# A set-attention and mixture-of-experts kernel: a listed order, output weights in the x buffers, later outputs of two batches, small steps on ScalarE or GpSimd

## The chip, the cores and the metric

The kernel runs on one core of one Trainium2 chip. The metric is device microseconds (us) of one execution, the median of several. Engines are called by the names of the profile: PE (TensorE), DVE (VectorE), ACT (ScalarE), POOL (GpSimd) and SP (SyncE, whose queue issues the transfers).

## The reference

`x` is 4 batches of 11456 tokens with 128 channels in float32, `inducing` is 32 rows of 128 channels. What is computed, cut to what matters:

```
def mab(q, kv):
    s = scale * (q @ kv.transpose(0, 2, 1))
    s = s - s.max(-1, keepdims=True)
    a = np.exp(s)
    a /= a.sum(-1, keepdims=True) + 1e-09
    return a @ kv
h = mab(I, x)             # 32 inducing rows attend over all tokens of a batch
out = mab(x, h)           # every token attends over the 32 rows h
# then, with x = out as 45824 rows:
do_compute = x @ w_skip > 0
e_idx = argmax(x @ w_gate); gate_w = softmax(x @ w_gate)[e_idx]
out[do_compute] = x + gate_w * (relu(x @ w1[e_idx]) @ w2[e_idx])
```

## The kernel before, in words

Tokens lie along the free dimension, channels on the 128 partitions. A batch is cut into six groups g0 to g5 of 2048 tokens (the short one has 1216; it comes first in batch 0 and last in the others), and a group into four quarters (`Q`), so that a tile of 128 partitions holds four quarters of 32 inducing rows. For each batch b there are these steps:

- **load** (L372): SP issues two transfers of 512 KB for each group of x.
- **first pass**, for each pair of groups: scores (L403, PE), their maximum (L407, DVE), exponentials (L413, ACT), transposes of these weights (L422, PE) and a copy out of PSUM; transposes of x (L438, PE, 8 at a time) and a copy (`xt`, on ACT at L354 or on DVE at L356); the weighted sum of x (L452, PE), added up on DVE (L461).
- **middle**, once in a batch, a chain of small steps: L504 to L534 make the normalised `hr` (L527 is its matmul, L532 the reciprocal before it), L537 transposes it, L543 copies it as `hc`; from `hc` come the logits of the 32 rows (L553, L554), the batch's expert (`choose`, L563 to L568), `lrq` (`seven`, L599 to L605), and through the expert's weights (`w1s`, `w2s`, loaded by SP after it has read the expert's number) `g` (L613, L620), signs (L635 to L639) and `yr` (L657 to L672).
- **second pass**, for each pair of groups, here called a unit: scores with `hc` (L754, PE), 32x32 block transposes into `e` (L758, DVE), softmax (L762 and L777 on DVE, L773 on ACT; `less` L770 and `norm` L783 as two halves on DVE or POOL), a transpose back into `u1` (L789); the expert's logits (L797, PE; `lt`, L806 and L807, DVE), `qexp` (L812, L813, ACT), `claim` (L817 to L820, POOL), the gates (L825, L826 on DVE, `pick` L829 on POOL, L834 on PE, a copy `gs` on ACT or DVE), `scale2` (L845, halves on DVE or POOL) and a second transpose back into `u2` (L789).
- **emit**, for each group: 8 matmuls with `hr` and `u1` and 8 with `yr` and `u2` (L885, PE, into two PSUM pairs), two copies `o` (ACT, or DVE), two stores (L894, SP). Below, one emit is a full one (2048 tokens) or a short one (1216).
- **marking** (L915 to L942), small, feeds a check at the end that decides whether tokens with another expert have to be added; in the profiled execution it found nothing to add.

No engine reorders its work. What stands in which order is made when the kernel is built: every step is an `Op` with a cost on each engine that may run it, buffers that it takes and frees, and a rank. `in_order` is a list scheduler: it goes through the steps by the time at which they could start, takes the lowest rank first among those within 0.1 us, picks the engine that would end first, and hands out the buffers. `best_order` starts from ranks by formula (for a group, `b * NG + g`, for its second pass `LEAD` more) and tries 4000 random changes of them, keeping what ends earlier by the planner's costs. The program is written in the order found; the waits come from the buffers. Where the planner sees PE idle for over 0.7 us, `awake` and `idle` put in transposes of the identity that nobody reads (L1124), which I call fillers.

Buffers: 11 for x (one holds a group), 3 for `u1`, 1 for `u2`, 4 for `o`, and five PSUM homes, three of which are pairs.

Of the kernel before, what the change touches and what calls it, by code (L numbers as in the profile page):

```python
# [22 lines left out]
HOMES = (2, 2, 2, 1, 1)  # L23


class Group:
# [1149 lines left out]
```

## Time and profile before

| | |
|---|---|
| median of 3 runs | 223.78 us (223.65 to 223.88) |
| the profiled execution | 222.58 us |
| its span, first to last instruction | 220.6 us |
| PE, DVE, ACT, POOL busy | 90%, 73%, 59%, 39% of the span |
| last matmul ends | 212.5 us |
| last store issued | 214.6 us |

The busy share is a mean over stages with different limits, so the stages are to be read one by one; a good cut are the four `hr` matmuls (L527), at 37.45, 74.22, 114.75 and 165.70 us of the span. PE's share counts the fillers as work.

### The profile page before, as it was taken

What the parts mean: (1) busy time and instruction counts of PE and PEld (TensorE: products, weight loads), DVE (VectorE), ACT (ScalarE), POOL (GpSimd) and SP (SyncE); (2) the same over time, 40 slices, a digit from 0 to 9 for tenths busy, and PEclk for the clock granted to TensorE, in tenths of its full rate; (3) what the DMA queues carried; (4) which work ended last, traced back from release to release, by engine and by line L of the source; (5) the groups of instructions that cost most, each with busy time, mean ns of one, the idle gap of its engine ahead of it and who ended that gap; (6) DMA issues with size and microseconds to landing.
All of it is one profiled execution on the core that took longest, in us unless ns stands there. A gap on an engine that the chain in (4) does not pass through costs nothing.

```text
span 220.6 us, 6196 instructions
## 1 busy us (share of the span) xinstructions
PE 199.2 (90%) x2535; PEld 125.6 (57%) x2536; DVE 161.1 (73%) x330; ACT 129.9 (59%) x183; POOL 86.7 (39%) x156
## 2 busy tenths in 40 slices
PE   6899999999999999999999989999988999786840
PEld 5478767764666876854657555445734236652420
DVE  0135306799999788288799998899998999999400
ACT  2365564716769855966948473566956553165650
POOL 6000000026285207333631576418672572983400
PEclk9999999999999999999999999999999999999996
DMA  6999950089920459909988937445227796008693
GB/s 161 398 416 408 408 237 0 3 278 413 408 87 3 192 132 386 360 7 361 352 297 269 357 144 243 195 189 229 83 95 288 223 390 265 0 24 360 247 348 110
DMA packets 16613, 51.63 MB, mean 234 GB/s; under 512 B 1984, under 2 KB 4928, under 8 KB 16576
## 3 DMA queue, kind: packets, MB, share of 16 engines
q1 hardware_dynamic: 16288, 51.12, 61.8%
q8 instruction: 22, 0.36, 0.7%
q14 instruction: 15, 0.12, 0.2%
q10 hardware_dynamic: 288, 0.02, 0.1%
HBM read 27.68 MB, written 23.46 MB: 232 GB/s over the span
## 4 chain that ended last, share of the span: by engine, by line
PE 42%; DVE 37%; DMA 5%; ACT 5%; issue 5%; POOL 3%; SPq 1%; ACTq 0%; DVEq 0%; POOLq 0%
PE bank L438 12%; PE bank L885 7%; DVE u L789 7%; PE bank L403 6%; PE bank L754 5%; DVE sums L777 5%; PE bank L452 4%; DVE e L758 3%; PE bank L422 3%; DMA x<-in_xT_dram 3%; DVE ts L762 3%; DMA out_dram<-o 2%; DVE mins L407 2%; DVE e L783 2%; DVE lt L806 1%
## 5 line engine op out<-in xcount | busy, mean ns | idle before, releaser
L354 ACT COPY o<-bank 128x1024 f32<-128x1024 f32 (+1 forms) x45 | 41.5, 954 | 15.9 <-PE bank L885 13.4
L438 PE MATMUL bank<-ident,x 128*128 128x128 f32 (+1 forms) x368 | 48.8, 277 | 1.0 <-DMA x<-in_xT_dram 0.5
L354 ACT COPY xt<-bank 128x1024 f32<-128x1024 f32 (+1 forms) x41 | 40.4, 996 | 15.8 <-PE bank L438 15.5
L438 PEld LDWEIGHTS bank<-ident,x 128*128 128x128 f32 (+1 forms) x368 | 40.6, 140 | 7.0 <-issue 2.4
L770 POOL TENSOR_TENSOR e<-e,ts 128x512 f32<-128x512 f32 (+1 forms) x19 | 20.6, 1093 | 58.3 <-DVE ts L762 58.3
L407 DVE TENSOR_REDUCE mins<-bank 128x1 f32<-128x1024 f32 (+3 forms) x13 | 13.7, 1056 | 23.4 <-PE bank L403 23.3
L789 DVE STREAM_TRANSPOSE u<-e 128x1024 f32<-128x1024 f32 (+1 forms) x24 | 28.3, 1186 | 2.8 <-PE bank L885 1.5
L783 POOL TENSOR_TENSOR e<-texp,ts 128x512 f32<-128x512 f32 (+1 forms) x19 | 20.2, 1073 | 23.0 <-DVE ts L779 15.0
L885 PE MATMUL bank<-u,hr 32*128 32x512 f32 (+1 forms) x192 | 26.0, 611 | 1.3 <-ACT o L354 1.1
L452 PE MATMUL bank<-xt,a1T 128*32 128x129 f32 (+1 forms) x736 | 25.3, 275 | 0.1
L452 PEld LDWEIGHTS bank<-xt,a1T 128*32 128x32 f32 (+1 forms) x736 | 19.5, 109 | 9.1 <-issue 6.3
L885 PE MATMUL bank<-u,yr 32*128 32x512 f32 (+1 forms) x192 | 23.5, 558 | 0.0
L403 PE MATMUL bank<-x,iT_sb 128*32 128x512 f32 (+1 forms) x192 | 22.8, 566 | 0.3 <-DMA x<-in_xT_dram 0.2
L754 PE MATMUL bank<-x,hc 128*32 128x512 f32 (+1 forms) x192 | 22.1, 578 | 1.0 <-DVE e L758 0.5
L413 ACT ACTIVATE a<-bank,mins 128x1024 f32<-128x1024 f32 (+3 forms) x13 | 13.0, 997 | 15.0 <-DVE mins L410 12.3
L845 POOL TENSOR_TENSOR e<-e,gs 128x512 f32<-128x512 f32 (+1 forms) x15 | 17.2, 1158 | 6.9 <-ACT gs L354 5.8
L773 ACT ACTIVATE texp<-e 128x1024 f32<-128x1024 f32 (+1 forms) x12 | 12.4, 1030 | 8.4 <-POOL e L770 8.4
L777 DVE TENSOR_REDUCE sums<-texp 128x32 f32<-128x1056 f32 (+1 forms) x12 | 14.3, 1195 | 3.6 <-ACT texp L773 3.5
L354 ACT COPY a1T<-bank 128x1024 f32<-128x1024 f32 (+4 forms) x17 | 12.1, 735 | 6.8 <-PE bank L422 6.7
L758 DVE STREAM_TRANSPOSE e<-bank 128x1024 f32<-128x1024 f32 (+1 forms) x12 | 14.3, 1190 | 1.6 <-PE bank L754 1.2
L885 PEld LDWEIGHTS bank<-u,yr 32*128 32x128 f32 x192 | 9.8, 185 | 9.4 <-issue 7.8
L817 POOL TENSOR_SCALAR posm<-lt 128x32 f32<-128x32 f32 (+1 forms) x12 | 4.2, 353 | 24.8 <-DVE lt L806 24.8
(131 smaller groups left out, 262.9 us busy)
## 6 DMA issues: line engine op xcount, KB each, us to landing
x<-in_xT_dram SPq DMA_DIRECT2D x43, 512.0 KB, 8.4
out_dram<-o SPq DMA_DIRECT2D x40, 512.0 KB, 3.4
out_dram<-o SPq DMA_DIRECT2D x8, 304.0 KB, 4.4
w1s<-in_w_dram SPq DMA_DIRECT2D x4, 512.0 KB, 3.9
w2s<-in_w_dram SPq DMA_DIRECT2D x4, 512.0 KB, 5.0
x<-in_xT_dram SPq DMA_DIRECT2D x4, 152.0 KB, 2.7
x<-in_xT_dram SPq DMA_DIRECT2D x3, 96.0 KB, 5.2
iT_sb<-in_iT_dram ACTq DMA_DIRECT2D x1, 16.0 KB, 2.2
```

The costliest lines, as they stand in the source:

```text
L354: nc.scalar.copy(out=out, in_=in_)
L403: nc.tensor.matmul(ps[q * M:(q + 1) * M, off[i]:off[i] + G.w1], lhsT=iT_sb, rhs=s.x[g][:, G.s1[q]:G.s1[q] + G.w1], start=True, stop=True)
L407: nc.vector.tensor_reduce(out=bias if one else mins[:, 0:1], in_=st["ps"][:, 0:W], axis=AX.X, op=ALU.max, negate=True)
L438: nc.tensor.transpose(out=px[0:w, (j * Q + q) * P:(j * Q + q + 1) * P], in_=s.x[gs[i]][:, o:o + w], identity=ident)
L452: nc.tensor.matmul(ph[q * M:(q + 1) * M, 0:P + 1], lhsT=st["aT"][0:w, j, q * M:(q + 1) * M], rhs=xts[bx[i].idx][0:w, k, q, :], start=(j == ...
L754: nc.tensor.matmul(ps[q * M:(q + 1) * M, off[i]:off[i] + G.w2], lhsT=s.hc[:, 0:M], rhs=s.x[g][:, G.s2[q]:G.s2[q] + G.w2], start=True, stop ...
L758: nc.vector.transpose(out=st["e"], in_=st["ps"][:, 0:W])
L770: on(o).tensor_tensor(out=v, in0=v, in1=part(st["mx"], i), op=ALU.subtract)
L777: nc.vector.tensor_reduce(out=r, in_=ev(M + 1), axis=AX.X, op=ALU.add)
L783: on(o).tensor_tensor(out=blocks(st["e"], i), in0=texps[bex.idx][:, t0:t0 + Gs[i].nb, 0:M], in1=part(st["i"], i), op=ALU.mult)
L789: nc.vector.transpose(out=st[f"u{k}"][:, 0:W], in_=st["e"])
L885: nc.tensor.matmul(at(bp[q // 2])[:, p0:p0 + G.w1], lhsT=m[r, :], rhs=st[k][r, c], start=(k == "u1"), stop=(k == "u2"))
```

## The change

- The order is no longer searched. `placed` reads a rank, and for steps with a choice of engine a bias, from a list of numbers, one for each step (`RANKS`), and runs `in_order` once. It overwrites every rank that the formulas give, those with `LEAD`, `EL` and `LATE` too, so these constants have no effect of their own.
- The four `u` buffers are gone and there are 13 x buffers. A unit takes one x buffer for its `u1` and `u2` when `u1` is written and gives it back after its last emit. The planner hands out x buffers one by one (`rooms`) rather than in turn.
- The emits of the last two batches have a rank of their own (`LE`).
- Small steps: `dw` is one ACT instruction with a negated bias from POOL (L521 on DVE goes); the scaling of `hr`, the copies `hc`, `g`, `yp`, `yr` may run on ACT; `seven` has four instructions rather than five and may run on POOL; the row sum of `hc` is a step by itself, so that the second pass doesn't wait for it; `unsure` has one instruction less; `least` is a tensor_tensor.
- The short group's quarters of 304 tokens are cut into blocks of 102, 100 and 102 rather than 128, 128 and 48, and transposed 102 at a time.
- Fillers are written right before the step that follows the gap rather than behind the step ahead of it. On PE this is the same place.

```diff
-def best_order(ops, bufs, rounds):
...
+def placed(ops, bufs):
+    table = RANKS.split()
+    assert len(table) == len(ops)
+    for o, v in zip(ops, table):
+        rank, _, spare = v.partition("/")
+        o.rank, o.spare = int(rank) / 100.0, int(spare or 0) / 10.0
+    done, end = in_order(ops, bufs)
+    assert end < math.inf
+    return done
...
+            elif b.tag == "x":
+                ends = [0.0 if v is None else v.end for v in rooms]
+                lo = min(v for v in ends if v is not None)
+                b.idx = max((v, i) for i, v in enumerate(ends) if v is not None and v <= max(t, lo))[1]
+                rooms[b.idx] = b
...
-        self.tb = [(c, min(P, self.w1 - c)) for c in range(0, self.w1, P)]
+        n = -(-self.w1 // P)
+        self.wb = -(-self.w1 // n)
+        at = [min(c, self.w1 - self.wb) for c in range(0, n * self.wb, self.wb)] + [self.w1]
+        self.tb = [(c, d - c) for c, d in zip(at, at[1:])]
...
-    XB = min(11, 2 * NG)
+    XB = min(13, 2 * NG + 2)
-    LEAD = NG + 4
+    LEAD = NG + 1
-    BUFS = {"x": XB, "a1": 2, "a1T": 1, "xt": 2, "e": 3, "u1": 3, "u2": 1, "lt": 2, "o": 4, "w": 1, "gsel": 1, "ex": 2}
+    BUFS = {"x": XB, "a1": 2, "a1T": 1, "xt": 2, "e": 3, "lt": 2, "o": 4, "w": 1, "gsel": 1, "ex": 2}
+    LATE = B - 2
+    EL = 4
...
-            nc.vector.tensor_tensor(out=d, in0=st["bb"][:, 0:1], in1=s.bias, op=ALU.subtract)
...
+            nc.scalar.activation(out=d, in_=st["bb"][:, 0:1], func=AF.Exp, bias=st["top"])
...
-            nc.vector.tensor_copy(out=s.hc[:, 0:P], in_=pt[:, 0:P])
-            nc.vector.tensor_reduce(out=s.hc[:, P:P + 1], in_=pt[:, 0:M], axis=AX.X, op=ALU.add)
-        s.o_hc = o = L.add({"DVE": 0.5}, columns, o, free=[f])
+            copy(o, s.hc[:, 0:P], pt[:, 0:P])
+        def whole(o):
+            nc.vector.tensor_reduce(out=s.hc[:, P:P + 1], in_=s.hc[:, 0:M], axis=AX.X, op=ALU.add)
+        s.o_hc = o = L.add({"DVE": 0.28, "ACT": 0.29}, columns, o, free=[f])
+        o = L.add({"DVE": 0.25}, whole, o)
...
-        s.o_lrq = L.add({"DVE": 0.89}, seven, o)
+        s.o_lrq = L.add({"DVE": 0.75, "POOL": 1.3}, seven, o)
...
-        b1, b2 = Buf("u1"), Buf("u2")
+        bu = Buf("x")
+        LE = Steps(L.rank + (EL if b >= LATE else 0))
...
+            u = st[f"u{k}"] = xs[bu.idx][:, (k - 1) * PW:k * PW]
+            nc.vector.transpose(out=u[:, 0:W], in_=st["e"])
...
-            o = emit(s, g, G, off[i], st, L, (o_1, o_2, o), [b1, b2] if i == len(gs) - 1 else [])
+            o = emit(s, g, G, off[i], st, LE, (o_1, o_2, o), [bu] if i == len(gs) - 1 else [])
...
-        done = best_order(all_steps(), BUFS, 4000)
+        done = placed(all_steps(), BUFS)
```

Where instructions now stand, at three places. In the rows, `hr_1_...` is `hr` of batch 1 and so on; in the changed kernel `u1` and `u2` are called x, since they lie in x buffers; L942 there is L885 of before, L891 is L834, L854 is L797, L1180 is L1124.

PE behind the transpose of batch 3's `hr`, up to the first scores of its second pass, before:

```order
L537 MATMUL bank3_73<-ident_80,hr_3_2270 128x128
L885 MATMUL bank2_72<-u1_2_2_1987,hr_2_1615 128x512 x2
L885 MATMUL bank0_70<-u1_2_2_1987,hr_2_1615 128x512 x2
L885 MATMUL bank2_72<-u2_2_2_2252,yr_2_1901 128x512 x2
L885 MATMUL bank0_70<-u2_2_2_2252,yr_2_1901 128x512 x2
L553 MATMUL bank4_74<-ws_sb_78,hc_3_2288 128x8
L554 MATMUL bank4_74<-ws_sb_78,hc_3_2288 128x9
L754 MATMUL bank1_71<-x_3_0_1459,hc_3_2288 32x512 x4
```

and in the changed kernel:

```order
L594 MATMUL bank4_71<-ident_77,hr_3_2138 128x128
L942 MATMUL bank2_69<-x6_154,hr_1_1031 128x304 x2
L942 MATMUL bank0_67<-x6_154,hr_1_1031 128x304 x2
L942 MATMUL bank2_69<-x6_154,yr_1_1280 128x304 x2
L942 MATMUL bank0_67<-x6_154,yr_1_1280 128x304 x2
L982 MATMUL bank3_70<-lom_2_2136,ones_82 128x1
L613 MATMUL bank4_71<-ws_sb_75,hc_3_2159 128x8
L614 MATMUL bank4_71<-ws_sb_75,hc_3_2159 128x9
L942 MATMUL bank2_69<-x9_157,hr_1_1031 128x512 x2
L942 MATMUL bank1_68<-x9_157,hr_1_1031 128x512 x2
L942 MATMUL bank2_69<-x9_157,yr_1_1280 128x512 x2
L942 MATMUL bank1_68<-x9_157,yr_1_1280 128x512 x2
```

Before, batch 2's third group is emitted here and batch 1 is long done; now a short and a full emit of batch 1 stand here. Counted to the end of the order, 10 emits stood behind this place (4 of batch 2, one of them short, and 6 of batch 3, one short), and now 15 do (3 of batch 1, one short, and 6 each of batches 2 and 3, one short each).

PE around the gates of batch 3's first unit, before:

```order
L797 MATMUL bank1_71<-u1_3_0_2306,lrq_3_163 32x128 x8
L668 MATMUL bank3_73<-yp_3_2481,rep_100 128x128
L1124 MATMUL bank2_72<-ident_80 128x128 x41
L834 MATMUL bank3_73<-lt_3_0_2472,rep_100 32x32 x4
L797 MATMUL bank3_73<-u1_3_2_2377,lrq_3_163 32x128 x8
L1124 MATMUL bank2_72<-ident_80 128x128 x15
L885 MATMUL bank0_70<-u1_3_0_2306,hr_3_2270 128x512 x2
```

and in the changed kernel:

```order
L854 MATMUL bank4_71<-x11_159,lrq_3_173 32x128 x8
L726 MATMUL bank3_70<-yp_3_2355,rep_97 128x128
L942 MATMUL bank0_67<-x1_149,hr_2_1632 128x512 x2
L942 MATMUL bank2_69<-x1_149,hr_2_1632 128x512 x2
L942 MATMUL bank0_67<-x1_149,yr_2_1880 128x512 x2
L942 MATMUL bank2_69<-x1_149,yr_2_1880 128x512 x2
L1180 MATMUL bank3_70<-ident_77 128x128 x7
L942 MATMUL bank0_67<-x1_149,hr_2_1632 128x304 x2
L942 MATMUL bank1_68<-x1_149,hr_2_1632 128x304 x2
L942 MATMUL bank0_67<-x1_149,yr_2_1880 128x304 x2
L942 MATMUL bank1_68<-x1_149,yr_2_1880 128x304 x2
L891 MATMUL bank4_71<-lt_3_0_2373,rep_97 32x32 x4
```

Where 41 fillers stood, a full and a short emit of batch 2 and 7 fillers stand now. In the whole program the fillers go from 78 to 32, not counting the 13 that both have ahead of the first transfer.

ACT in the last unit of batch 3, from `qexp` to the copy of the gates, before:

```order
L812 ACTIVATE qexp1_124<-lt_3_4_2636 128x28x7
L813 ACTIVATE qexp1_124<-qexp1_124 128x28x7
L354 COPY o_3_2_0_2674<-bank0_70 128x1024
L354 COPY gs2_1_148<-bank3_73 128x28
L354 COPY o_3_2_1_2683<-bank1_71 128x1024
```

and in the changed kernel:

```order
L869 ACTIVATE qexp1_121<-lt_3_4_2521 128x28x7
L870 ACTIVATE qexp1_121<-qexp1_121 128x28x7
L401 COPY o_3_1_0_2560<-bank0_67 128x1024
L401 COPY o_3_1_1_2566<-bank1_68 128x1024
L401 COPY o_3_2_0_2588<-bank0_67 128x1024
L401 COPY gs2_1_145<-bank4_71 128x28
```

One output copy stood ahead of the last gates, and now three do.

## Rows read from the trace of the kernel before

**Rows 1.** The page: busy time of the engines over the span, then the slices of PE, of its granted clock and of the transfers (40 slices of 5.5 us, tenths).

```profile
PE 199.2 (90%) x2535; PEld 125.6 (57%) x2536; DVE 161.1 (73%) x330; ACT 129.9 (59%) x183; POOL 86.7 (39%) x156
...
PE   6899999999999999999999989999988999786840
...
PEclk9999999999999999999999999999999999999996
DMA  6999950089920459909988937445227796008693
```

**Rows 2.** Busy time of each engine between the four `hr` matmuls, from the first matmul on x to the end; the columns are stretch, length, busy time (and instructions) of PE, its weight loads, DVE, ACT and POOL, then granted clock, share of the transfer engines, GB/s.

```profile
4.40:37.45 33.05, 32.09 (x403) 21.33 (x403) 10.61 (x19) 17.72 (x25) 0.00 (x0) 1.00 0.81 320
37.45:74.22 36.77, 36.26 (x516) 24.69 (x513) 33.50 (x70) 23.72 (x34) 15.72 (x21) 1.00 0.50 191
74.22:114.75 40.53, 39.80 (x548) 26.07 (x547) 30.39 (x67) 27.18 (x37) 15.86 (x23) 1.00 0.74 266
114.75:165.70 50.95, 48.28 (x646) 29.00 (x644) 48.24 (x94) 33.36 (x48) 26.66 (x39) 1.00 0.54 201
165.70:212.50 46.80, 39.93 (x424) 21.63 (x420) 38.35 (x82) 25.10 (x35) 24.90 (x39) 1.00 0.61 232
212.50:220.60 8.10, 0.00 (x0) 0.00 (x0) 0.00 (x0) 1.33 (x2) 0.00 (x0) 0.79 0.54 194
```

**Rows 3.** PE's timeline from batch 3's `hr` matmul to the end (start, length, then the instructions; in brackets the idle time before).

```profile
165.70 0.49 PE L527 MATMUL bank<-acc,rep 128*128 128x129 f32 x2
...
168.11 1.14 PE L885 MATMUL bank<-u,hr 32*128 32x512 f32 x8
...
170.04 0.39 PE L553 MATMUL bank<-ws_sb,hc 128*128 128x8 f32 x2
...
180.40 0.79 PE L885 MATMUL bank<-u,hr 32*128 32x304 f32 x8 [0.48 <-ACT o L354]
...
181.64 0.44 PE L626 MATMUL bank<-ident,g 128*128 128x128 f32 x2
...
185.89 4.64 PE L1124 MATMUL bank<-ident 128*128 128x128 f32 x41
191.10 0.27 PE L834 MATMUL bank<-lt,rep 128*32 128x32 f32 x8 [0.57 <-POOL lt L829]
```

**Rows 4.** Groups of instructions by line and shape over the whole span (count, busy time, mean of one in ns, then idle time before).

```profile
L354 ACT COPY o<-bank 128x1024 f32<-128x1024 f32 x37 | 36.3, 1016 | 13.5 <-PE bank L885 12.2 <-issue 1.2
...
L1124 PE MATMUL bank<-ident 128*128 128x128 f32 x78 | 9.9, 276 | 0.0
...
L845 POOL TENSOR_TENSOR e<-e,gs 128x512 f32<-128x512 f32 x12 | 14.4, 1200 | 6.2 <-ACT gs L354 5.0 <-DVE gs L356 1.1
...
L845 DVE TENSOR_TENSOR e<-e,gs 128x512 f32<-128x512 f32 x8 | 8.6, 1069 | 1.5 <-ACT gs L354 1.5
...
L356 DVE COPY xt<-bank 128x1024 f32<-128x1024 f32 x5 | 6.1, 1225 | 2.1 <-PE bank L438 2.1
...
L356 DVE COPY o<-bank 128x1024 f32<-128x1024 f32 x3 | 3.6, 1197 | 0.2 <-PE bank L885 0.2
...
L783 DVE TENSOR_TENSOR e<-texp,ts 128x512 f32<-128x512 f32 x3 | 2.9, 973 | 0.0
...
L620 DVE COPY g<-bank 128x256 f32<-128x256 f32 x4 | 1.6, 399 | 0.0
...
L605 DVE TENSOR_TENSOR lrq<-r,cmask 128x32 f32<-128x32 f32 x4 | 1.4, 338 | 0.2
...
L665 DVE COPY yp<-bank 128x128 f32<-128x128 f32 x4 | 1.1, 287 | 1.9 <-PE bank L834 1.4 <-PE bank L657 0.5
```

**Rows 5.** Busy time, columns as in the second group, in three stretches of the end: from batch 3's reciprocal (L532) to its first `e` transpose (L758), from there to the last `lt` (L806), and from there to the end of the last `u2` transpose (L789).

```profile
167.24:173.74 6.50, 5.89 (x57) 2.75 (x61) 5.43 (x27) 3.33 (x6) 3.37 (x9) 1.00 0.66 250
173.74:201.95 28.21, 23.88 (x265) 13.69 (x261) 27.30 (x42) 13.63 (x19) 17.75 (x24) 1.00 0.54 198
201.95:208.20 6.25, 4.79 (x51) 2.20 (x47) 4.05 (x13) 4.07 (x7) 3.79 (x8) 1.00 0.72 290
```

**Rows 6.** The last unit's gates, from the timeline of all engines: POOL's `pick` (L829), its matmul (L834), the copy of the gates, DVE's half of `scale2` (L845), and the two marking steps (L938, L939) that POOL runs behind the pick.

```profile
204.21 0.48 POOL L829 TENSOR_TENSOR lt<-lt,gs 128x112 f32<-128x112 f32 x1 [0.32 <-DVE gs L826]
204.66 0.46 POOL L938 TENSOR_SCALAR gxs<-gxs 128x96 f32<-128x96 f32 x1
204.75 0.16 PEld L834 LDWEIGHTS bank<-lt,rep 128*32 128x32 f32 x8 [2.11 <-POOL lt L829]
...
205.08 0.18 ACT L354 COPY gs<-bank 128x28 f32<-128x28 f32 x1 [0.57 <-PE bank L834]
...
205.19 0.39 POOL L939 TENSOR_TENSOR gxs<-gxs,posm 128x96 f32<-128x96 f32 x1
205.29 0.83 DVE L845 TENSOR_TENSOR e<-e,gs 128x512 f32<-128x512 f32 x1 [1.22 <-ACT gs L354]
```

**Rows 7.** The x loads (the line L372), time from issue to landing.

```profile
DMA to landing us min/median/max: 2.3/8.0/11.3
```

**Rows 8.** The granted clock of PE around the end of its work, columns as in the second group.

```profile
214.00:216.00 2.00, 0.00 (x0) 0.00 (x0) 0.00 (x0) 0.59 (x1) 0.00 (x0) 1.00 0.78 280
216.00:218.00 2.00, 0.00 (x0) 0.00 (x0) 0.00 (x0) 0.00 (x0) 0.00 (x0) 0.80 0.57 197
218.00:220.60 2.60, 0.00 (x0) 0.00 (x0) 0.00 (x0) 0.00 (x0) 0.00 (x0) 0.50 0.03 9
```

More of the change, by code (lines that the diff above doesn't have):

```diff
@@ L298 @@
     xts = [const.tile([P, GC // Q // P, Q, P + 1], F32, name=f"xt{i}") for i in range(BUFS["xt"])]
+    xs = [const.tile([P, GC], F32, name=f"x{i}") for i in range(XB)]
     for t in xts:
@@ L389, in first @@
         tb = [(i, k, c, w) for i, G in enumerate(Gs) for k, (c, w) in enumerate(G.tb)]
-        nt, full = len(tb), sum(w == P for *_, w in tb)
+        nt = len(tb)
+        runs = [(sum(len(H.tb) for H in Gs[:i]), len(G.tb), G.wb) for i, G in enumerate(Gs)]
+        if n == 2 and Gs[0].wb == Gs[1].wb:
+            runs = [(0, nt, Gs[0].wb)]
         mins = None if one else s.mins
@@ L409, in least @@
         def least(o):
[L410 removed]
+            nc.vector.tensor_tensor(out=bias, in0=mins[:, 0:1], in1=old, op=ALU.min)
         def exps(o):
@@ L425, in aTc @@
             pa, t = st["pa"], st["aT"]
-            if full:
-                copy(o, t.rearrange("p t c -> p (t c)")[:, 0:full * P], pa[:, 0:full * P])
-            if full < nt:
-                w = tb[-1][3]
-                copy(o, t[0:w, full, :], pa[0:w, full * P:(full + 1) * P])
+            for j, k, w in runs:
+                copy(o, t.rearrange("p t c -> p (t c)")[0:w, j * P:(j + k) * P], pa[0:w, j * P:(j + k) * P])
         def xt(i, ks, buf):
@@ L467, in first @@
         if not one:
-            o = L.add({"DVE": 0.27}, least, o, s.lastm)
+            o = L.add({"DVE": 0.17}, least, o, s.lastm)
         s.lastm = o
@@ L619, in g_rows @@
             gr = st["g4"] = wk.tile([P, F // Q], F32, tag="g4", bufs=1, name=f"g4_{b}")
-            nc.vector.tensor_copy(out=gr, in_=st["gr"][:, 0:F // Q])
-        o = L.add({"DVE": 0.44}, g_rows, o, free=[f])
+            copy(o, gr, st["gr"][:, 0:F // Q])
+        o = L.add({"DVE": 0.44, "ACT": 0.4}, g_rows, o, free=[f])
         def g_columns(pg):
@@ L664, in parts @@
             yp = st["y4"] = wk.tile([P, P], F32, tag="yp", bufs=1, name=f"yp_{b}")
-            nc.vector.tensor_copy(out=yp, in_=st["yp"][:, 0:P])
-        o = L.add({"DVE": 0.28}, parts, o, free=[f])
+            copy(o, yp, st["yp"][:, 0:P])
+        o = L.add({"DVE": 0.28, "ACT": 0.29}, parts, o, free=[f])
         o, f = mm(0.22, FULL, lambda p: nc.tensor.matmul(p[:, 0:P], lhsT=rep, rhs=st["y4"], start=True, stop=True), "y", o)
@@ L671, in rows @@
             s.yr = perb.tile([P, P], F32, tag="yr", name=f"yr_{b}")
-            nc.vector.tensor_copy(out=s.yr, in_=st["y"][:, 0:P])
-        s.o_yr = L.add({"DVE": 0.25}, rows, o, free=[f])
+            copy(o, s.yr, st["y"][:, 0:P])
+        s.o_yr = L.add({"DVE": 0.25, "ACT": 0.29}, rows, o, free=[f])
         return L
@@ L847, in second @@
         units = list(enumerate(zip(gs, Gs)))
-        o = last["s2"] = L.add(pe(W), scores, s.o_hc, last["s2"], take=[bs, be, b1], free=[s.xbuf[g] for g in gs], **TILE)
+        o = last["s2"] = L.add(pe(W), scores, s.o_hc, last["s2"], take=[bs, be], free=[s.xbuf[g] for g in gs], **TILE)
         o = L.add(dve(W), tokens, o, free=[bs])
@@ L1126 @@
     with tc.manual_schedule():
-        done = best_order(all_steps(), BUFS, 4000)
+        done = placed(all_steps(), BUFS)
         more = awake(done)
-        pes = [o for o in done if o.eng == "PE"]
-        before = {a: more[b] for a, b in zip(pes, pes[1:]) if b in more}
         for o in done:
+            if o in more:
+                idle(*more[o])
             o.fn(o)
-            if o in before:
-                idle(*before[o])
     others()
```

150 lines of the change are left out of this document (89 added, 61 removed).

## The prediction

> **What bounds the kernel now.** I read the page's slices first: PE is at nine tenths nearly throughout, and at its end stands a stretch in which the transfers are idle for two slices [rows 1]. A busy PE may be running fillers, so I then cut the span at the four `hr` matmuls [rows 2]. The reader is to see three regimes there. Up to the third cut (114.75 us) PE has work for all but 0.96 + 0.51 + 0.73 us, and DVE has time left: this is PE's. From 114.75 to 165.70 PE is busy 48.28 and DVE 48.24 of 50.95 us: both are full. In the last 46.80 us PE is busy 39.93, but 74 of the 78 fillers lie here, at 9.9 / 78 = 0.127 us each [rows 4], so 9.4 us of that is nothing; real work is 30.5, waits 6.9. DVE has 38.35. The timeline shows the emptiest place, 41 fillers after 185.89 and a wait for POOL until 191.10 [rows 3]. The end is thus a chain: batch 3's second pass, which can start only after its `hr`, goes through DVE with little beside it for PE to do. The cut of that stretch says so too: between the first `e` and the last `lt` DVE is busy 27.30 of 28.21 us, in the last unit only 4.05 of 6.25 [rows 5].
>
> So the time is: when batch 3's `hr` matmul runs (165.70), then 46.80 us to the last matmul, then 8.10 us of copies and stores.
>
> **The sum.** *PE ahead of batch 3's `hr`.* The number of real matmuls doesn't change. But 15 emits stand behind that `hr` and not 10: four full and one short move from before it to after it. A full emit takes 170.04 - 168.11 = 1.93 us, a short one 181.64 - 180.40 = 1.24 [rows 3]: 4 x 1.93 + 1.24 = 9.0 us less PE work ahead. The four fillers at the start go too: 0.5. The 4.87 us in which PE waits in these four stretches [rows 2] I leave as they are. The `hr` then comes at 165.7 - 9.5 = 156.2 us.
>
> *DVE ahead of it* must follow, since it was as full as PE in the fourth stretch. Counted in the order, DVE loses: `norm` halves, from 3 of 512 and 2 of 384 to 2 of 512 (0.97, the smaller ones about 0.74), 2.4 us; `scale2`, from 8 of 512 to 5, one of 384 more (1.07), 2.7; `o` copies, 3 to 1 (1.20), 2.4; `xt` copies, 5 to 3 full ones and two narrow ones of the short group for two others, 1.9; the small copies `g`, `hc`, `yp`, `yr`, 16 to 6 (0.40, others about 0.29), 3.0; `seven` (whose last instruction means 0.34), half of them on POOL and one instruction less in the others, about 2.6; L521 and one of `unsure`, 1.1; one scaling of `hr`, 0.3. It gains six `a1T` copies of 1024, 512 and 384 columns, priced as `xt` at 1.22 for 1024: 4.9. That is 11 us net in row means; since records overlap, I count 161.1 / 177 of it, 10 us (177 is the sum of the row means, 161.1 the busy time) [rows 1, 4]. Nearly all of it lies ahead of batch 3's `hr`: from its reciprocal on, DVE has 40 us of row means in either order. So DVE gives 10 where PE gives 9.5, and PE's 9.5 stands.
>
> A rule of the Trainium skill would take DVE alone here. Perfetto Trace Analysis, Identifying the Most-Contended Engine, says that matmul busy time is a bad measure and that TensorE's headroom is to be judged by its weight loads (and FLOPs); by these, 57% against DVE's 73% [rows 1], DVE would be the bound everywhere, the `hr` would come 10 us earlier and my sum be 0.5 lower. The stretches speak for the row: in the third, weight loads fill 26.07 of 40.53 us and DVE 30.39, yet PE stood still for 0.73 [rows 2].
>
> *Where the work goes.* POOL takes 1 + 2 more `norm` halves, 3 more `scale2` halves of 512 (1.20) for one of 384, two `seven` and four negations: some 9 us on an engine with 86.7 of 220 busy [rows 1]. It is hidden, except in the last unit (below). ACT gets about 2 us more. The blocks of 102 tokens save nothing: the same number of transposes and copies, where a copy is narrower or wider by tens of columns.
>
> *The end, from batch 3's reciprocal.* First `e` transpose: 6.50 us behind it before [rows 5]. Now a short and a full emit and the logits stand on PE ahead of those scores, where a full emit stood, which is 1.2 us later on PE; `seven` is gone from DVE's queue, but a `scale2` half and two `u2` transposes are in it, row means of 7.2 us for 6.0. I take 6.9. From there to the last `lt`: 27.0 us of DVE row means instead of 28.9, the stretch is DVE's, so 28.2 - 1.8 = 26.4. The last unit: 6.25 before. POOL now has a `scale2` half of another unit (1.20) ahead of `claim`, and the two marking steps (0.46 + 0.39), which ran behind the pick, ahead of it [rows 6]: 2.05 later. ACT then has three output copies ahead of the gates and not one, at 1.02 each [rows 4], and one of them is likely to be running: up to 1.0 more. I take 2.9, near the upper bound of 3.1, since both queues are in order; below, zero if the waits overlap. So 6.9 + 26.4 + 9.1 = 42.4 for 41.0: the tail is 1.4 longer.
>
> Does PE fit? Real work 30.5 + 9.0, and 32 fillers, 4.1, make 43.6 of 48.2 us; 4.6 remain for waits, where there were 6.9. That is what the emits are moved for: they stand in the places of fillers. ACT: 25.1 + 8 x 1.02 + 2 x 0.67 = 34.6 of 48. Transfers: 12 full and 3 short emits and the weights are 15.5 MB in 56 us, 276 GB/s, where the third stretch moved 266 and had spells of ten tenths [rows 1, 2]. It fits if it isn't bunched; I keep the 8.10.
>
> *x buffers.* The least distance from the last scores that read a buffer to the first ones of its next load is 10 us of PE work, once; the others have over 11. A load lands 8.0 us after its issue, 11.3 at most [rows 7]. Cost 0, at worst 1.3.
>
> Sum: 156.2 + 46.8 + 1.4 + 8.1 = 212.5 us of span for 220.6, so 8.1 less. The profiled execution was 222.58, so 214.5 for it; the median of the runs shown is 1.2 above that one, so **215.7 us**.
>
> **The rivals.** *The tail keeps its waits.* The emits fill the fillers' places but meet other waits (for ACT's copies, for `o` buffers), and the 6.9 us stay: 43.6 + 6.9 + 8.1 behind 156.2 is 214.8, so 218.0. For it: POOL and ACT queues are longer and every engine runs in order. Against: most of those waits were for the chain.
>
> *It goes better.* With 10 us less on DVE, half of the 4.87 us ahead of the `hr` vanish and the tail gets no longer: 153.8 + 54.9 = 208.7, so 211.9.
>
> *PE's clock falls; slower.* There are 46 fillers fewer, and they are all that PE does in some gaps. The trace shows a granted clock of 1.00 through the whole program, though with gaps [rows 2]; it falls to 0.80 on average and then to 0.50, the level of 1.2 GHz, only after PE has run nothing since 212.5 [rows 8]. If it fell ahead of the last eight emits, 7 x 1.93 + 1.24 = 14.8 us of matmuls would take twice that; less the 4.6 us of waits that it would cover, the end would come 10.2 later: 222.7, so 225.9. It decides from 12.7 us of work at the low level on. Against: PE has more real work in the tail than before. TensorE: Matmul & The Clock Gate, HAM oscillation, in the Trainium skill, states that a wait between bursts of matmuls can throttle the clock so that each burst begins cold; by that, taking fillers out speaks against this change, and the trace of before shows no such fall between its bursts.
>
> *The list does nothing.* The constants that rank the emits later are overwritten, and the same order could have come out; but the two orders differ at each of the places read, so only a tail longer by 8 us would give 223.8.
>
> **How the numbers follow.** My forecast 0.57; the tail keeps its waits 0.20; better 0.16; no change 0.03; slower 0.04. The range for 8 in 10 reaches from the better case, 211.8, to beyond the kept waits by the 1.3 us of a late load, 219.6. A measurement here can tell about 0.2% from no change. Faster by more than that: 0.93; within: 0.03; slower: 0.04.
>
> **What would show it.** Right: the fourth `hr` matmul at 155 to 157.5 us, the third within 1.5 us of 114.75, the last matmul at about 204.4; DVE busy near 151 and fillers 4.1 us. If the fourth `hr` is later than 160, the DVE or PE term failed; if it is early and the last matmul after 206, the waits of the tail came back; a granted clock under 1 before 200 would be the third rival. A PE wait for an x load after 60 us would show that the buffers are too few.

## The result and the profile after

| | before | after |
|---|---|---|
| median, us | 223.82 (4 runs, 223.65 to 223.88) | 213.63 (4 runs, 213.21 to 214.81) |
| the profiled execution, its span | 222.58, 220.6 | 213.21, 211.5 |
| the four `hr` matmuls | 37.45, 74.22, 114.75, 165.70 | 38.48, 73.96, 115.52, 154.18 |
| last matmul ends | 212.50 | 203.77 |

The change is faster: the ratio is 0.9555, 95% interval 0.9516 to 0.9593. The forecast was 215.7 us, within 211.8 to 219.6. Three of all the executions below were slow ones, one of the kernel before (494.65 us) and two of `x_own_u_search` (223.22 and 223.44 us), and they are left out of the medians and ratios.

The page of the kernel after, as [rows 1]: busy times, then the slices of PE, its granted clock and the transfers.

```profile
PE 193.4 (91%) x2489; PEld 122.9 (58%) x2490; DVE 153.4 (73%) x297; ACT 132.0 (62%) x190; POOL 92.5 (44%) x173
...
PE   7999999999999999999999899999999979879850
...
PEclk9999999999999999999999999999999999999995
DMA  5999996049690049609993069202576994888893
```

The stretches between the `hr` matmuls, columns as in [rows 2]:

```profile
4.40:38.48 34.08, 33.45 (x408) 23.22 (x408) 12.20 (x22) 17.26 (x23) 0.25 (x1) 1.00 0.91 360
38.48:73.96 35.48, 34.67 (x482) 23.45 (x480) 28.89 (x55) 22.05 (x31) 13.80 (x20) 1.00 0.47 168
73.96:115.52 41.56, 40.73 (x596) 27.32 (x595) 37.98 (x77) 28.67 (x44) 24.75 (x41) 1.00 0.68 244
115.52:154.18 38.66, 37.27 (x525) 24.96 (x523) 35.52 (x70) 26.33 (x39) 19.78 (x31) 1.00 0.40 150
154.18:203.77 49.59, 44.37 (x479) 21.32 (x475) 38.84 (x75) 34.91 (x50) 30.37 (x48) 1.00 0.81 309
203.77:211.50 7.73, 0.00 (x0) 0.00 (x0) 0.00 (x0) 1.23 (x2) 0.00 (x0) 0.62 0.56 199
```

Set against [rows 2], the fourth stretch has shrunk from 50.95 to 38.66 us, with PE's work there down from 48.28 to 37.27 and DVE's from 48.24 to 35.52. The third stretch, 40.53 us before, has become 41.56. What came back is in the last row but one: 46.80 has become 49.59, and the transfers, at 0.61 there before, are at 0.81.

The three stretches of the end, as [rows 5] (here the reciprocal is L582, the first `e` L816, the last `lt` L863, the last `u2` L846):

```profile
154.90:162.37 7.47, 6.95 (x91) 3.78 (x87) 6.44 (x21) 5.09 (x10) 4.40 (x6) 1.00 0.66 236
162.37:189.47 27.10, 24.14 (x274) 10.79 (x267) 25.61 (x43) 19.31 (x28) 20.38 (x33) 1.00 0.82 315
189.47:198.86 9.39, 8.12 (x73) 4.12 (x72) 6.28 (x11) 6.64 (x11) 5.35 (x9) 1.00 0.90 353
```

The last unit's gates, as [rows 6], from the timeline of all engines (L994 and L995 are the marking steps, L886 `pick`, L891 its matmul):

```profile
192.91 0.45 POOL L994 TENSOR_SCALAR gxs<-gxs 128x96 f32<-128x96 f32 x1
...
193.44 0.39 POOL L995 TENSOR_TENSOR gxs<-gxs,posm 128x96 f32<-128x96 f32 x1
...
193.78 0.48 POOL L886 TENSOR_TENSOR lt<-lt,gs 128x112 f32<-128x112 f32 x1
...
194.04 1.04 PE L942 MATMUL bank<-x,yr 32*128 32x512 f32 x8
...
195.11 1.01 ACT L401 COPY o<-bank 128x1024 f32<-128x1024 f32 x1 [1.17 <-PE bank L942]
...
195.33 0.26 PE L891 MATMUL bank<-lt,rep 128*32 128x28 f32 x8
...
196.02 0.19 ACT L401 COPY gs<-bank 128x28 f32<-128x28 f32 x1
...
196.28 1.43 POOL L902 TENSOR_TENSOR e<-e,gs 128x512 f32<-128x512 f32 x1 [2.02 <-ACT gs L401]
```

From the end of `pick` (194.26) to the gates' copy are now 1.76 us, where they were 0.39 [rows 6]: PE is in the middle of an emit, and ACT in an output copy. The emits, though, are late themselves. PE's timeline, the first matmuls of three of the last emits:

```profile
193.08 1.14 PE L942 MATMUL bank<-x,hr 32*128 32x512 f32 x8 [0.18 <-ACT o L401]
...
196.18 1.14 PE L942 MATMUL bank<-x,hr 32*128 32x512 f32 x8 [0.59 <-ACT o L401]
...
199.32 1.14 PE L942 MATMUL bank<-x,hr 32*128 32x512 f32 x8 [0.23 <-ACT o L401]
```

They follow each other every 3.1 us, where the matmuls of one take 2.1; each ends its wait with an output copy (ACT `o`), since an emit needs two of three PSUM pairs. The waits in brackets are short because other matmuls, and two blocks of seven fillers (198.11 and 201.25 us), fill most of that 1 us. Over the whole span, PE's waits for output copies have grown (total us, times, longest), first before, then after:

```profile
PE bank L885 <- ACT o L354: 1.1, 4, 0.5
```

```profile
PE bank L942 <- ACT o L401: 3.5, 10, 0.6
```

### The profile page after: what moved, and what is told of

Its sections match the earlier page's. It is cut to its first block, busy times and chain, and to the rows that moved or that the text cites. A ratio compares the mean times of both kernels' runs of the same rounds, so it can differ in the third digit from the quotient of the medians.

```text
span 211.5 us, 6113 instructions
## 1 busy us (share of the span) xinstructions
PE 193.4 (91%) x2489; PEld 122.9 (58%) x2490; DVE 153.4 (73%) x297; ACT 132.0 (62%) x190; POOL 92.5 (44%) x173
## 4 chain that ended last, share of the span: by engine, by line
PE 20%; DVE 20%; ACT 7%; POOL 2%; issue 2%; ACTq 0%; DVEq 0%
PE bank L942 14%; ACT o L401 6%; DVE x L846 3%; DVE ts L820 3%; DVE e L816 3%; PE bank L486 2%; DVE sums L835 2%; DVE mins L457 2%; DVE e L902 1%; PE bank L500 1%; PE bank L812 1%; POOL e L902 1%; PE bank L854 1%; POOL e L828 1%; DVE gs L883 1%
## 5 line engine op out<-in xcount | busy, mean ns | idle before, releaser
L401 ACT COPY xt<-bank 128x1024 f32<-128x1024 f32 (+2 forms) x43 | 41.7, 988 | 6.7 <-PE bank L486 5.9
L846 DVE STREAM_TRANSPOSE x<-e 128x1024 f32<-128x1024 f32 (+1 forms) x24 | 28.5, 1186 | 2.0 <-POOL e L902 1.3
L942 PE MATMUL bank<-x,hr 32*128 32x512 f32 (+1 forms) x192 | 26.0, 611 | 3.9 <-ACT o L401 3.5
L841 POOL TENSOR_TENSOR e<-texp,ts 128x512 f32<-128x512 f32 (+1 forms) x22 | 22.5, 1034 | 13.6 <-DVE lo L972 5.0
L500 PE MATMUL bank<-xt,a1T 128*32 128x129 f32 (+2 forms) x736 | 26.0, 274 | 0.0
L500 PEld LDWEIGHTS bank<-xt,a1T 128*32 128x32 f32 (+2 forms) x736 | 21.1, 110 | 7.8 <-issue 5.3
L942 PE MATMUL bank<-x,yr 32*128 32x512 f32 (+1 forms) x192 | 23.5, 558 | 0.0
L902 POOL TENSOR_TENSOR e<-e,gs 128x512 f32<-128x512 f32 (+1 forms) x17 | 19.1, 1136 | 5.9 <-ACT gs L401 5.5
L816 DVE STREAM_TRANSPOSE e<-bank 128x1024 f32<-128x1024 f32 (+1 forms) x12 | 14.2, 1187 | 5.3 <-PE bank L812 4.4
L942 PEld LDWEIGHTS bank<-x,yr 32*128 32x128 f32 x192 | 9.9, 185 | 9.3 <-issue 8.9
L820 DVE TENSOR_REDUCE ts<-e 128x32 f32<-128x1024 f32 (+1 forms) x12 | 13.8, 1152 | 0.0
```

The source lines that it names most:

```text
L401: nc.scalar.copy(out=out, in_=in_)
L500: nc.tensor.matmul(ph[q * M:(q + 1) * M, 0:P + 1], lhsT=st["aT"][0:w, j, q * M:(q + 1) * M], rhs=xts[bx[i].idx][0:w, k, q, :], start=(j == ...
L816: nc.vector.transpose(out=st["e"], in_=st["ps"][:, 0:W])
L820: nc.vector.tensor_reduce(out=mx[:, 0:nb], in_=blocks(st["e"]), axis=AX.X, op=ALU.max)
L841: on(o).tensor_tensor(out=blocks(st["e"], i), in0=texps[bex.idx][:, t0:t0 + Gs[i].nb, 0:M], in1=part(st["i"], i), op=ALU.mult)
L846: nc.vector.transpose(out=u[:, 0:W], in_=st["e"])
```

## The experiments

All are made from the kernel after, but for one from the kernel before. The kernel before ran beside each group, at 222.68, 223.01 and 223.04 us, and the kernel after again beside the last. Medians of different groups were taken on different chips, so the ratio to the kernel before is the safer comparison.

**A part alone, a part undone, and the order found as before.**

`x_search`: the list is not read.

```diff
-        done = placed(all_steps(), BUFS)
+        done = best_order(all_steps(), BUFS, 4000)
```

> The changed kernel, but its order comes from the 4000 random trials of the kernel before, with the ranks written in the code (LEAD of NG + 1, outputs of batches 2 and 3 four places later), and not from the list. Sixteen emits stand behind batch 3's hr matmul, one more than with the list. Theory A (what counts is how many emits may lie behind that hr, which the shared buffers allow): the hr at 152 to 156 us, the time 213 to 217 us. Theory B (DVE's smaller load counts): the same 213 to 217, since the edits on DVE are in. Theory C (the list itself counts, its order waits less than a found one): 220 to 225 us, the waits of PE ahead of the fourth hr at 6 us or more, where the list has 3.7.

`x_own_u_search`: as that, with buffers for `u1` and `u2` of their own.

```diff
-    XB = min(13, 2 * NG + 2)
+    XB = min(11, 2 * NG)
...
-        bu = Buf("x")
+        bu = {1: Buf("u1"), 2: Buf("u2")}
...
```

> As the run with the random trials, but the output weights u1 and u2 have three and one buffers of their own again and x has 11. The second u2 can then be written only after the emits of the unit before it have read the first. Ten emits stand behind batch 3's hr, as in the kernel before; all edits on DVE, ACT and POOL stay. Theory A: 5 to 6 more emits ahead of the hr at 1.93 us, so the hr 9 to 11 us later than with shared buffers (163 to 166 us), the tail about 3 shorter, the time 6 to 8 us above the run with the random trials and shared buffers. Theory B: no later hr, within 1.5 us of that run. Theory C: both are within 2 us of each other, near 222.

`b_xbuf`: the kernel before, with the shared buffers (13 x buffers, handed out one by one), `LEAD` and the ranks of the late outputs alone.

```diff
...
-        b1, b2 = Buf("u1"), Buf("u2")
+        bu = Buf("x")
+        LE = Steps(L.rank + (EL if b >= LATE else 0))
...
```

> The kernel before with one part of the change alone: u1 and u2 share one x buffer (13 in all), LEAD is NG + 1 and the outputs of batches 2 and 3 rank four places later; the order is found by the 4000 random trials. All small steps stay on DVE, the blocks stay 128/128/48. Fourteen emits stand behind batch 3's hr. Theory A: PE has 4 emits, 7.7 us, less ahead of that hr and the time is 216 to 218 us. Theory B (DVE was as full as PE in the fourth stretch, 48.24 of 50.95 us, and binds as soon as PE's emits are gone): at most 2 us gained, 221 to 224. Theory C: 222 to 226.

`x_small_dve`: the list's order, the small steps on DVE.

```diff
         more = awake(done)
+        for o in done:
+            if o.fn.__name__ in ("hrs", "columns", "g_rows", "parts", "rows", "seven"):
+                o.eng = "DVE"
```

> The changed kernel in its own order (the list), but after the order is made the scaling of hr, the copies hc, g, yp and yr and the steps of seven all go to DVE: 11 small copies at 0.25 to 0.44 us and two more seven of about 1.3 us, some 5 us of DVE in all, 4 of them ahead of batch 3's hr. If DVE binds there as PE does (the prediction's 10 us for 9.5), the hr is 3 to 4 us later and the time 216 to 218 us. If PE alone binds after the change, 213.5 to 214.5 us.

Measured, with PE's work (fillers too) and waits from 4.40 us to the fourth `hr`, and the tail from there to the last matmul (of the profiled execution):

| kernel | emits behind `hr` | PE works, waits | `hr` | tail | median, us | ratio to before |
|---|---|---|---|---|---|---|
| before | 10 | 156.43, 4.87 | 165.70 | 46.80 | | 1 |
| x_own_u_search | 10 | 155.15, 4.85 | 164.40 | 48.80 | 220.36 | 0.9904 (0.9868 to 0.9940) |
| b_xbuf | 14 | 151.41, 7.07 | 162.88 | 47.34 | 219.71 | 0.9851 (0.9809 to 0.9893) |
| x_search | 16 | 145.46, 8.08 | 157.94 | 52.96 | 219.85 | 0.9859 (0.9822 to 0.9896) |
| x_small_dve | 15 | 146.83, 5.86 | 157.09 | 51.64 | 218.81 | 0.9837 (0.9775 to 0.9898) |
| after | 15 | 146.12, 3.66 | 154.18 | 49.59 | 213.63 | 0.9555 (0.9516 to 0.9593) |

The tail of x_own_u_search can't be set beside the others: it is that of an execution of 223.22 us, with a granted clock of 0.93 there; ahead of its `hr` the clock was 1.00. The stretches of x_search, columns as in [rows 2]:

```profile
4.40:38.88 34.48, 32.79 (x412) 22.46 (x411) 13.08 (x21) 17.47 (x25) 0.25 (x1) 1.00 0.91 355
38.88:74.52 35.64, 34.13 (x474) 23.68 (x473) 26.75 (x52) 22.93 (x35) 13.83 (x18) 1.00 0.46 167
74.52:116.84 42.32, 38.70 (x556) 24.61 (x554) 35.02 (x69) 27.93 (x40) 18.60 (x28) 1.00 0.59 198
116.84:157.94 41.10, 39.84 (x567) 26.47 (x563) 39.09 (x75) 27.79 (x44) 24.08 (x39) 1.00 0.41 149
157.94:210.90 52.96, 48.16 (x500) 22.78 (x496) 41.60 (x82) 35.58 (x51) 29.23 (x46) 1.00 0.83 316
```

Theory A is right on PE's work and wrong on the time. With the buffers shared, the emits do go behind the `hr` (10 become 14 or 16; undone, they are 10 again, and that `hr` is 6.5 us later than in x_search, but the time only 0.5), and PE has 5 to 11 us less ahead of it. But in a found order 2 to 3 us of that return as waits (of x_search's 8.08 us, 3.62 lie in the third row, where the kernel before has 0.73), and in x_search the tail takes 6 more. In found orders the parts don't add up: the shared buffers alone are worth 3.0 us (b_xbuf), all edits but these buffers and the list 2.3 (x_own_u_search), and both together 2.8 (x_search). With the buffers shared, the smaller load of DVE gives a found order nothing.

In the list's order the same small steps are worth 5.2 us (218.81 to 213.63, and 6 by the ratios): with them on DVE the `hr` is 2.9 later and the tail 2.1 longer. And the list without them is no clear gain on b_xbuf: 218.81 for 219.71, with intervals that overlap. So list and small steps are worth much only together. Theory C named the waits rightly, but was 0.2 off with its 220; b_xbuf's 219.71 lies in none of its three ranges, and x_small_dve's time is 0.8 above the range given for it.

Two things stay open. Each found order is one result of one random search (a fixed seed), and how far another seed would land from it was not measured, so differences of 1 or 2 us between found orders may be chance. And x_small_dve keeps a list that was made with these steps on other engines; a list made for them on DVE might lose less than 5 us.

**Which engine is full.** `x_dve_dose`:

```diff
-            nc.vector.tensor_reduce(out=mx[:, 0:nb], in_=blocks(st["e"]), axis=AX.X, op=ALU.max)
+            for _ in range(2 if b < B - 1 else 1):
+                nc.vector.tensor_reduce(out=mx[:, 0:nb], in_=blocks(st["e"]), axis=AX.X, op=ALU.max)
```

> The changed kernel in its own order, with the maxima of the second pass (1.198 us for 1024 columns, 1.059 for 896) issued twice in batches 0 to 2: 6 x 1.198 + 3 x 1.059 = 10.4 us more on DVE, all ahead of batch 3's end, some 8 to 10 of it ahead of its hr matmul. If DVE binds after the change as PE does: 7 to 10 us more, 221 to 224 us. If DVE only sets the tail and PE binds ahead of the hr: 0 to 3 us more, since DVE was idle for 14 of 150 us there.

`x_pe_dose`:

```diff
-            for i, (g, G) in enumerate(zip(gs, Gs)):
+            for i, (g, G) in [v for v in enumerate(zip(gs, Gs)) for _ in range(2 if b < B - 1 and W == PW else 1)]:
```

> The changed kernel in its own order, with the scores of the second pass (1.71 us for two full groups) issued twice in the six full units of batches 0 to 2: 6 x 1.71 = 10.3 us more on PE. The prediction has PE as the bound up to batch 3's hr: 8 to 10 us more there, 222 to 224 us. If DVE alone binds since the change: at most the 3.7 us of PE's waits are filled first, 6 us or less more. Both doses costing nearly their size would say that both engines bind, each at its places.

223.28 and 223.63 us (ratios to before 1.0008, 0.9977 to 1.0039, and 1.0034, 1.0008 to 1.0060): 9.7 and 10.0 us above the kernel after. The third and fourth stretch, first with DVE's dose, then with PE's:

```profile
76.25:122.78 46.53, 42.51 (x596) 27.75 (x595) 41.46 (x79) 28.37 (x43) 25.54 (x41) 0.96 0.61 218
122.78:164.85 42.07, 37.99 (x525) 24.95 (x523) 39.14 (x74) 26.75 (x39) 19.55 (x31) 1.00 0.38 138
```

```profile
78.54:123.28 44.74, 43.94 (x629) 28.16 (x627) 38.18 (x76) 28.49 (x43) 24.72 (x41) 1.00 0.63 227
123.28:164.84 41.56, 40.61 (x557) 25.98 (x555) 35.49 (x71) 26.56 (x39) 19.69 (x31) 1.00 0.37 138
```

The `hr` comes at 164.85 and 164.84, 10.7 later in both. PE's dose of 10.3 us is filled into no wait. DVE's 10.4 is not hidden either, though DVE stood still for 13.3 us between the first `hr` and the fourth in the kernel after (3.6 and 3.1 of them in these two stretches). The cleanest row is the fourth, at a clock of 1.00 in all three kernels: 3.6 us more of DVE made it 3.4 longer, and 3.3 us more of PE 2.9. In the third, part of DVE's price is PE's clock, which fell to 0.96 in the mean behind a long wait:

```profile
111.66 2.05 PE L943 MATMUL bank<-x,hr 32*128 32x512 f32 x8 [2.15 <-DVE xt L403]
```

The same 596 matmuls kept PE busy for 1.8 us more there, so of the 10.7 some 8.9 are DVE's own. Neither engine has room, then. That DVE's gaps can't be used because the two engines wait for each other through the chain of a unit is argued and not shown: both doses lengthen a step of that chain, and no run lengthens one engine's work beside it.

**Fillers, widths and the end.** `x_nofill`:

```diff
-        more = awake(done)
+        more = {}
```

> The changed kernel in its own order without the 32 fillers. If PE's clock needs them: a granted clock under 1 in the tail and up to 10 us more. If not: the clock stays at 1.00 up to the last matmul and the time is 213 to 214.5 us; a filler that stands just ahead of work that has come free could even cost a few tenths.

213.79 us, ratio 0.9595 (0.9561 to 0.9629): no change in the median. But the profiled execution took 216.2, and its clock did fall. PE's timeline of that kernel, then the stretch from there (columns as in [rows 2]):

```profile
179.21 0.79 PE L942 MATMUL bank<-x,hr 32*128 32x304 f32 x8 [1.10 <-ACT o L401]
...
181.27 2.09 PE L942 MATMUL bank<-x,hr 32*128 32x512 f32 x8 [0.55 <-ACT o L401]
183.14 1.79 PE L942 MATMUL bank<-x,yr 32*128 32x512 f32 x8
```

```profile
181.20:183.00 1.80, 1.73 (x8) 0.87 (x12) 1.80 (x3) 1.57 (x4) 1.62 (x2) 0.52 0.99 369
```

Behind two waits, of 1.10 and 0.55 us, PE ran one emit near the level of 1.2 GHz, 3.66 us instead of 2.1, and the clock was back at 1.00 by 185. So the third rival's mechanism exists; it costs 1.6 us in an execution in which it happens, not 10, and the other four (213.34 to 213.86) show no such loss. Fillers aren't all that decides: x_tail_a and x_tail_b (below) have none behind that `hr` either, and the same two waits of 1.10 and 0.55 us; the clock of the first fell there in its profiled execution, that of the second didn't.

`x_half2`: batch 3's emits by halves.

```diff
-            for k, m in (("u1", s.hr), ("u2", s.yr)):
-                for q in range(Q):
+            late = b == B - 1
+            for h, k, m in [(h, k, m) for h in ((0, 2) if late else (0,)) for k, m in (("u1", s.hr), ("u2", s.yr))]:
+                for q in (range(h, h + 2) if late else range(Q)):
...
-        m = L.add(..., take=bp, free=done, **ROWS)
+        m = L.add(..., take=bp[::-1] if b == B - 1 else bp, free=done, **ROWS)
```

> The changed kernel in its own order, but the six emits of batch 3 are written by halves: first both matmuls (u1 and u2) of the half whose pair of banks is free, then those of the other half, so that the first output copy can start when half of the emit is done. In the tail of the changed kernel the emits follow each other every 3.1 us (196.18, 199.32, 202.46), which is 2.1 of matmuls and one output copy of 1.0 that the next emit waits for. Theory D (this wait sets the pace): 2.2 to 2.7 us an emit, the last matmul 1 to 2 us earlier, the time 211.5 to 212.5. Theory E (the transfers set it: an emit's 1.05 MB at the 330 to 350 GB/s of this stretch is 3.0 to 3.2 us): 213 to 214, the same. Theory F (with two row groups side by side and not four each emit is longer): 214 to 216.

214.36 us (212.35 to 215.45), ratio 0.9604 (0.9533 to 0.9675): the same. Where both halves could run, they ran side by side, and the first copy still came at the end of the emit. PE and ACT there:

```profile
200.80 1.15 PE L943 MATMUL bank<-x,hr 32*128 32x512 f32 x8
201.76 1.05 PE L943 MATMUL bank<-x,yr 32*128 32x512 f32 x8
202.74 0.98 PE L1181 MATMUL bank<-ident 128*128 128x128 f32 x7
203.65 0.81 PE L943 MATMUL bank<-x,hr 32*128 32x304 f32 x6
```

```profile
202.87 1.93 ACT L401 COPY o<-bank 128x1024 f32<-128x1024 f32 x2 [1.21 <-PE bank L943]
```

What now stands ahead of the last emit is a block of seven fillers (L1181), made for a wait that the halves had taken away. So this run decides neither for D nor for E. Of F, longer emits, in whose range the median lies, the trace shows little: two emits whose second half started 0.3 us late took 2.3 us (194.87 to 197.21, 197.65 to 199.96). The last two runs keep the halves and take these fillers away too. `x_again` is the kernel after, unchanged; `x_uneven`:

```diff
-        self.wb = -(-self.w1 // n)
+        self.wb = P
...
```

> The changed kernel as it is, on the same chip as the three runs beside it: 213 to 214.5 us, the level against which these are read.

> The changed kernel in its own order, but the short group's three blocks are 128 tokens wide again (the middle one uses 48 of its 128 rows), with the same number of transposes and copies as with 102. By the prediction the even blocks save nothing: within 0.5 us of the changed kernel. If the width of a block counts: 26 columns more in each of 48 x transposes and 12 of a1 is 1560 columns, at 128 columns in 0.14 us some 1.7 us of PE, and up to 1.7 us longer.

`x_tail_a`, on top of `x_half2`, without the fillers behind batch 3's `hr` (these are 32, all there are, and not 28):

```diff
         more = awake(done)
+        more = {o: v for o, v in more.items() if o.at < 150.0}
```

> As the run with batch 3's emits by halves, and without the 28 fillers that stand behind batch 3's hr. In that run three blocks of seven fillers stood directly ahead of emits whose banks were free by then (194.87, 200.80, 203.65 us), at 0.9 us each, and the last unit's gates ran behind the first of these emits. Theory G (those fillers and the wait for a copy were all that held the emits): each of the last emits starts when the one before ends, the last matmul at 202 to 203 us, the time 211.5 to 212.5. Theory E (the transfers are the bound of the last 25 us): the last matmul is earlier and the copies and stores behind it take so much longer, 213 to 214 us.

`x_tail_b`, on top of that, with the second output copies of the last unit's two emits and its copy of the gates on DVE:

```diff
...
+        for o in copies[-2:] + gates[-1:]:
+            o.eng = "DVE"
```

> As the run without those fillers, and DVE, which is idle behind the last u2, takes the second output copies of the last unit's two emits and the copy of its gates. Theory G: the gates 0.2 us earlier, the last copy 0.6 to 1.0 us earlier, 210.8 to 212 us. Theory E: no further change, 213 to 214.

| kernel | median, us | ratio to before | `hr`, last matmul |
|---|---|---|---|
| x_again | 213.53 | 0.9569 (0.9543 to 0.9596) | 154.17, 203.74 |
| x_uneven | 214.41 | 0.9621 (0.9599 to 0.9643) | 154.83, 204.42 |
| x_tail_a | 213.41 | 0.9569 (0.9531 to 0.9608) | 154.53, 203.95 |
| x_tail_b | 212.63 | 0.9540 (0.9507 to 0.9572) | 154.70, 202.42 |

The even blocks are worth 0.9 us, 214.41 for 213.53, with intervals that barely miss each other. PE's work in the second to fourth stretch is 113.72 us with wide blocks, and 112.67 to 112.93 in the six profiled executions with narrow ones and the same order there. x_tail_b is the lowest of all, but 0.9 us against x_again is not settled: the intervals overlap. It beats the kernel before by 4.6%. Its stretches from 190 us on, and its timeline of ACT:

```profile
190.00:195.00 5.00, 4.45 (x32) 2.28 (x32) 3.97 (x7) 4.13 (x8) 3.92 (x8) 1.00 1.00 390
195.00:200.00 5.00, 4.77 (x44) 2.34 (x46) 2.09 (x5) 3.53 (x4) 1.42 (x1) 1.00 0.90 354
200.00:205.00 5.00, 2.40 (x22) 1.18 (x17) 2.02 (x2) 1.68 (x2) 0.00 (x0) 1.00 1.02 394
```

```profile
194.58 1.01 ACT L401 COPY o<-bank 128x1024 f32<-128x1024 f32 x1 [0.70 <-DMA out_dram<-o]
...
201.96 0.67 ACT L401 COPY o<-bank 128x608 f32<-128x608 f32 x1 [0.89 <-DMA out_dram<-o]
```

Here some output copies wait for stores to give their buffers back, with the transfers at 0.90 to 1.02, as theory E has it. By these medians the waits for copies are worth 1 us at most; that more needs stores that start earlier is argued, and was not tried. x_tail_a's time is in E's range (213 to 214), x_tail_b's between G's and E's. In x_tail_a's profiled execution the clock fell as in x_nofill (0.50 from 181.2 to 183.0), so its 203.95 says little of theory G.

## Why the prediction was right, and where it was off

- **PE ahead of the `hr`**: forecast 9.5 us less work, measured 156.43 - 146.12 = 10.3, and 9.3 to 10.0 in the five other profiled executions with the same order there (x_again, x_nofill, x_half2, x_tail_a, x_tail_b). The emits and early fillers are as forecast. "The blocks of 102 tokens save nothing" is wrong by 0.8 to 1.0 us of PE (x_uneven), no more than these executions differ by; what in PE it saves is not shown, since transposes of 102 and of 128 tokens both have a mean of 276 ns.
- **The 4.87 us of waits, left as they are**: they became 3.66, and x_search shows that they could have grown: 8.08. The prediction gave no reason for this term, so that it erred to the good side is luck. The `hr` came at 154.18 and not 156.2 (ahead of the 155 to 157.5 that was to show the forecast right): 0.8 of that is work and 1.2 is waits.
- **DVE gives 10**: row means fell by 8.9 and not 11, busy time by 7.7. That DVE must follow PE was right, and its price was near full: x_small_dve and x_dve_dose. The step that failed is to carry row means from one order to another. Three kinds of step came out dearer, by 2.6 us together: the running minimum (mean 0.27 us, where it was 0.15), `scale2` halves on DVE (1.21 for 1.07) and one of the steps of signs (L695, 0.56 for 0.37). But of the nine minima seven took 0.14 to 0.15 us and two 0.70 and 0.69. These two began while POOL ran a half of `less`, and ended 0.01 us behind it; one of them:

```profile
66.90 1.05 POOL L828 TENSOR_TENSOR e<-e,ts 128x512 f32<-128x512 f32 x1
...
67.26 0.70 DVE L460 TENSOR_TENSOR mins<-mins 128x1 f32<-128x1 f32 x1
```

  The same goes for all four L695 (0.38 to 0.93 us, each ending 0.02 us behind an instruction of POOL) and for the three long `scale2` halves (1.50 to 1.55 us, each ending 0.55 us behind one). So the price of such a step is set by what POOL is doing then.
- **The rule that DVE alone binds**: PE's dose of 10.3 us moved the `hr` by 10.7, with weight loads filling 25.98 of 41.56 us of the fourth stretch. By what the Trainium skill states (Perfetto Trace Analysis, Identifying the Most-Contended Engine), PE would be judged by these weight loads; the measurement decides against that here.
- **x buffers**: cost 0, as forecast. PE's only wait for an x load is 0.21 us at 5.80 us.
- **The tail**: forecast 6.9 + 26.4 + 9.1, measured 7.47 + 27.10 + 9.39, and from the `hr` to the last matmul 49.6 for 48.2. All three terms were too small, by 0.6, 0.7 and 0.3 us, and 0.2 came back beside them. The first was taken at 6.9 against its own two counts, by which PE and DVE each had 1.2 us more than the 6.50 of before; it became 7.47, and DVE stood still there for 1.03 us, as before (1.07). In the second, "the stretch is DVE's" is what failed: DVE stood still for 0.98 us ahead of the last `lt`, whose logits (L854) stood on PE behind one of the moved emits.

```profile
186.88 1.14 PE L942 MATMUL bank<-x,hr 32*128 32x512 f32 x8 [0.20 <-ACT o L401]
...
188.81 0.59 PE L854 MATMUL bank<-x,lrq 128*32 128x128 f32 x16
...
189.47 0.42 DVE L863 STREAM_TRANSPOSE lt<-bank 128x224 f32<-128x224 f32 x1 [0.98 <-PE bank L891]
```

  In the last unit the `pick` starts 4.31 us behind that `lt`, where it was 2.26: 2.05 later, as forecast for POOL's queue, though DVE's gates came at 193.67 and would have let it start only 0.1 earlier. Between the `pick` and the gates' copy 1.37 us were added, where the forecast had 0.85 for ACT's copies and nothing for PE being in an emit; 0.28 came back behind the copy.
- **The first rival** came in part: PE's waits of the tail, which the forecast put at 4.6 us, measured 49.59 - 44.37 = 5.2, with 44.37 of work for 43.6. Those for output copies, 1.1 us before, are 3.5, and those for the chain (POOL and DVE) have shrunk instead.
- **The rest**: 7.7 us behind the last matmul for 8.10, 1.7 between span and execution for 2.0, and a median 0.4 above the profiled execution and not 1.2. With -2.0 and +1.4 these make the 2.1 us between 215.7 and 213.63; the two large errors partly cancel.
- **Clock**: at 1.00 to the last matmul in the kernel after, as forecast. Without its fillers it fell behind waits of 1.10 and 0.55 us in two of three profiled executions, at 1.6 us in x_nofill, where the rival had 10. TensorE: Matmul & The Clock Gate, HAM oscillation, in the Trainium skill, says that waits between bursts of matmuls can make the next burst cold; x_nofill bears that out in kind.

## What to carry to other kernels

Where two engines have no room, as here, a change that relieves one can be worth nothing in one order (x_search against b_xbuf) and 5 us in another (x_small_dve against the kernel after): measure parts in pairs, and dose each engine to see which is full. A mean price taken from one order need not hold in another, if the step can meet another engine's. Buffers decide which orders are possible; look first at which buffer forces a step to stand early. Fillers are placed for the waits of one order, and have to be placed anew when the waits move.
